# Loading w1 in two pieces, the small one first, and moving eight wo products to later gaps of TensorE

## Chip, cores, metric

The kernel runs on one core of one Trainium2 chip. The metric is the device time of one execution in microseconds (us), the median of several runs.

## The reference

One token goes through a gated mix of an attention block and a dense block. Only the last 4096 of 32768 cached keys and values are read.

```python
def reference(A_x, A_k_cache, A_v_cache, A_wq, A_wo, B_x, B_w1, B_b1, B_w2, B_b2, gate_w):
    x = A_x                                        # [1, 1, 576]
    g = sigmoid((x * gate_w).sum(-1, keepdims=True))
    # A: 32 query heads, 16 KV heads of 128, window W = 4096
    q = x @ wq;  p = softmax(q @ k[-W:].T * 128 ** -0.5);  a = (p @ v[-W:]) @ wo
    # B: 576 -> 4608 -> 576
    b = gelu(x @ w1 + b1) @ w2 + b2
    return g * a + (1 - g) * b
```

K and V of the window are 16.8 MB each, wq, wo, w1 and w2 5 MB each: 53.6 MB are read for a single token. (The code above is shortened; the kernel passes x for both blocks.)

## The kernel before

The parts that matter. All large loads go through one DMA queue, issued by SyncE (SP) in the order in which they are used; four small rows (x, the gate weights, b2, b1) go through a second queue, issued by ScalarE (ACT). The first SP load is moved ahead of everything else in the program.

```python
    nc.scalar.dma_start(out=x_row, ...)            # 1.1 KB each; b1_t two rows of 4.6 KB
    nc.scalar.dma_start(out=gw_row, ...)
    nc.scalar.dma_start(out=b2_row, ...)
    nc.scalar.dma_start(out=b1_t, ...)

    w1_t = big.tile([P, NI, FH], BF16, name="w1_t", tag="B")      # 128 x 9 x 2304
    w1_src = B_w1.rearrange("d (h n) -> (d h) n", h=2).rearrange("(p i) n -> p i n", i=NI)
    nc.sync.dma_start(out=w1_t[:], in_=w1_src)     # one row of 41,472 bytes per partition
    wq_t = ...                                     # one row of 36,864 bytes per partition
    # ... [cut: constants, x2 = x spread over the partitions, the gate g] ...
    for j in range(NJ): ...                        # h_ps  = b1 (18 matmuls)
    for i in range(NI):                            # h_ps += w1 (162 matmuls), i outermost
        for j in range(NJ):
            nc.tensor.matmul(h_ps[:, j:NF:NJ], lhsT=w1_t[:, i, j:FH:NJ], rhs=x2[:, i, :], ...)
    # ... [cut: gelu -> gt; q = wq x; K loads and transposes, scores; softmax; V loads, o] ...
    for r0, r1 in ((0, 16), (16, RO)):             # RO = 32
        nc.sync.dma_start(out=wo_t[:, r0:r1, :], in_=wo_src[:, r0:r1, :])
    for j0, j1 in ((0, 10), (10, 16), (16, 18)):   # second half of w2
        nc.sync.dma_start(out=w2_t[:, NJ + j0 : NJ + j1, :], in_=w2_src[:, 1, j0:j1, :])
    # ... [cut] ... y_add makes two matmuls, one for each half of the 576 outputs
    with tc.issue_after(ov_mm.ins):
        for f in range(6, NJ):
            y_add(gt[:, f : f + 1], w2_t[:, f, :])
    for r in range(RO):
        y_add(ov[:, r : r + 1], wo_t[:, r, :])
    for f in range(NJ, NF):
        y_add(gt[:, f : f + 1], w2_t[:, f, :], stop=(f == NF - 1))
    # out_row <- y (ScalarE and VectorE, one half each), then the store
```

## Time and profile before

| | before |
|---|---|
| time, median of 4 runs | 133.07 us (132.94 to 133.3) |
| span of the profiled run | 131.0 us |
| main DMA queue | 53.61 MB, packets 96.4% of 16 engines' span |
| x row lands / b1 rows are used | 7.4 / 15.5 us |
| h_ps done, q_ps done | 28.0, 31.85 us |
| last K, last V, last waited-for w2 landing | 66.4, 111.5, 128.2 us |

The first lines to read are those of the page: the 40 equal slices of the span (3.3 us each; a digit is tenths of the busy share or of the granted clock) and the line of the main DMA queue.

```profile
PEclk9999999999999999999999965555555555556999
DMA  7999899899999999999999999999999989999980
GB/s 215 481 470 456 362 439 450 356 435 425 420 430 425 425 425 430 430 425 425 440 424 492 400 420 470 410 410 460 425 400 455 460 375 400 433 427 419 407 329 26
...
q1 hardware_dynamic: 2882, 53.61, 96.4%
```

The DMA row is full, or nearly so (8 or 9), from the second slice to the last but one. The rate of 425 to 430 GB/s in the middle lies close to the fabric ceiling of 435 GB/s that the Trainium skill gives ("DMA: Bandwidth & Descriptors", Specifications); this trace agrees with that figure. TensorE, the busiest engine, is at 59%.

Next the chain of work that ended last, in order of time (start, duration, what; only some of its 67 pieces):

```profile
1.91 13.59 DMA rows<-in_B_b_dram
...
15.54 1.27 PE h_ps L304 x18
16.82 1.05 PE y_ps L290 x4
17.86 10.14 PE h_ps L316 x162
28.00 3.85 PE q_ps L354 x144
...
32.45 33.94 DMA k_t<-in_A_k_cache_dram
...
101.27 26.86 DMA w_t<-in_B_w_dram
...
128.17 1.20 PE y_ps L290 x16
```

A chain names one releaser for each wait. It names TensorE work (h_ps, q_ps) between two long DMA stretches, which looks as though a faster h_ps would help. It would not: behind q_ps the chain waits for K until 66.4 us. That K load is issued at 32.4 us, when a buffer comes free, and then stands 34 us in the DMA queue behind the loads issued before it.

The end of the timeline (start, duration, engine, line, what, count, and in brackets the idle time before it with its releaser):

```profile
116.70 3.04 PE L290 MATMUL y_ps<-w_t,gt 128*1 128x288 bf16 x24
...
119.53 2.63 PE L290 MATMUL y_ps<-wo_t,ov 128*1 128x288 bf16 x32
122.61 2.12 PE L290 MATMUL y_ps<-wo_t,ov 128*1 128x288 bf16 x32 [0.45 <-DMA wo_t<-in_A_wo_dram]
...
126.07 1.39 PE L290 MATMUL y_ps<-w_t,gt 128*1 128x288 bf16 x20 [1.34 <-DMA w_t<-in_B_w_dram]
...
128.17 1.15 PE L290 MATMUL y_ps<-w_t,gt 128*1 128x288 bf16 x16 [0.70 <-DMA w_t<-in_B_w_dram]
...
129.35 0.45 DVE L534 CAST out_row<-y_ps 1x288 bf16<-1x288 f32 x1 [12.36 <-PE y_ps L290]
```

TensorE waits three times for data at the end: 0.45, 1.34 and 0.70 us. After the last wait 16 matmuls remain (1.15 us), then the copies and the store.

### The profile page before, as it was taken

Reading aid. Unit: us, or ns where it says so; the run is one execution under the profiler, and the core shown is the slowest. Engines: PE = TensorE matmul, PEld = TensorE weight load, DVE = VectorE, ACT = ScalarE, POOL = GpSimd, SP = SyncE. Lnnn points to the kernel's source line nnn. Section 1 sums busy time; section 2 is a strip of 40 time slices with the busy share of each in tenths; the row PEclk is TensorE's granted clock in tenths of the full one; section 3 lists DMA queues with packets and bytes.
Section 4 is the critical chain, followed back from the end, with each engine's and each line's share of the span. In section 5 each row is a group of like instructions: output and inputs, shape, how many; then the busy total and the mean of one; then the engine's idle time right before and its main releaser. Section 6 shows DMA issues by size and latency. Waiting matters only on the chain.

```text
span 131.0 us, 2371 instructions
## 1 busy us (share of the span) xinstructions
PE 77.3 (59%) x1126; PEld 44.7 (34%) x1062; DVE 51.8 (40%) x48; ACT 13.0 (10%) x25; POOL 5.6 (4%) x25
## 2 busy tenths in 40 slices
PE   0021299998599778768768220004934730999853
PEld 0011279997112111111111010004934730955521
DVE  0025600034988988988986620736000000010001
ACT  2100000001200000000000029960000000000001
POOL 5004600000000000000000000000000000000000
PEclk9999999999999999999999965555555555556999
DMA  7999899899999999999999999999999989999980
GB/s 215 481 470 456 362 439 450 356 435 425 420 430 425 425 425 430 430 425 425 440 424 492 400 420 470 410 410 460 425 400 455 460 375 400 433 427 419 407 329 26
DMA packets 2900, 53.75 MB, mean 410 GB/s; under 512 B 326, under 2 KB 330, under 8 KB 588
## 3 DMA queue, kind: packets, MB, share of 16 engines
q1 hardware_dynamic: 2882, 53.61, 96.4%
q8 instruction: 8, 0.13, 0.4%
q10 hardware_dynamic: 10, 0.01, 0.0%
HBM read 53.62 MB, written 0.00 MB: 409 GB/s over the span
## 4 chain that ended last, share of the span: by engine, by line
DMA 57%; PE 22%; DVE 8%; ACT 8%; issue 3%; SPq 1%; ACTq 1%; DVEq 0%
DMA k_t<-in_A_k_cache_dram 26%; DMA w_t<-in_B_w_dram 20%; DMA rows<-in_B_b_dram 10%; PE h_ps L316 8%; ACT p_t L449 7%; PE o_ps L493 5%; DVE kt L397 3%; PE q_ps L354 3%; DVE pt L457 2%; DVE m L419 2%; PE y_ps L290 2%; PE s_ps L407 1%; PE h_ps L304 1%; SPq L506 1%; PE t_ps L473 0%
## 5 line engine op out<-in xcount | busy, mean ns | idle before, releaser
L397 DVE STREAM_TRANSPOSE kt<-k_t 128x2048 f32<-128x2048 f32 x16 | 36.0, 2290 | 4.9 <-DMA k_t<-in_A_k_cache_dram 4.9
L407 PE MATMUL s_ps<-kt,qz_flat 128*128 128x512 bf16 x128 | 32.0, 397 | 8.6 <-DVE kt L397 8.6
L493 PE MATMUL o_ps<-pt,v_t 128*128 128x8 bf16 x512 | 14.5, 168 | 10.0 <-DMA v_t<-in_A_v_cache_dram 7.3
L407 PEld LDWEIGHTS <-qz_flat 128*128 128x128 bf16 x64 | 6.4, 99 | 33.6 <-issue 33.6
L493 PEld LDWEIGHTS <-v_t 128*128 128x128 bf16 x512 | 14.3, 105 | 10.3 <-DMA v_t<-in_A_v_cache_dram 7.5
L449 ACT ACTIVATE p_t<-s_ps,negm 128x512 bf16<-128x512 f32 x8 | 9.7, 1410 | 44.2 <-DVE negm L440 44.2
L316 PEld LDWEIGHTS <-w_t 128*128 128x128 bf16 x162 | 10.1, 160 | 1.0 <-issue 1.0
L316 PE MATMUL h_ps<-x,w_t 128*128 128x2 bf16 x162 | 10.2, 202 | 0.0
L511 DVE TENSOR_TENSOR om<-o_ps,rgh 128x128 bf16<-128x128 f32 x1 | 0.3, 291 | 23.6 <-PE o_ps L493 23.6
L290 PE MATMUL y_ps<-w_t,gt 128*1 128x288 bf16 x72 | 7.2, 362 | 2.0 <-DMA w_t<-in_B_w_dram 2.0
L473 PE MATMUL t_ps<-ls,ones 128*128 128x32 f32 x2 | 0.6, 396 | 12.7 <-DVE ls L471 12.7
L457 DVE STREAM_TRANSPOSE pt<-p_t 128x2048 bf16<-128x2048 bf16 x2 | 4.6, 2312 | 7.4 <-ACT p_t L449 7.4
L239 PE MATMUL xs_ps<-one_b,rows 1*128 1x1 bf16 x9 | 0.7, 196 | 8.2 <-DVE rows L233 8.2
L534 DVE CAST out_row<-y_ps 1x288 bf16<-1x288 f32 x1 | 0.4, 446 | 12.4 <-PE y_ps L290 12.4
L290 PEld LDWEIGHTS <-gt 128*1 128x1 bf16 x72 | 3.6, 99 | 4.6 <-issue 2.5
L325 DVE COPY hacc<-h_ps 128x36 f32<-128x36 f32 x1 | 0.2, 196 | 12.3 <-PE h_ps L316 12.3
L290 PE MATMUL y_ps<-wo_t,ov 128*1 128x288 bf16 x64 | 4.8, 306 | 0.4 <-DMA wo_t<-in_A_wo_dram 0.4
L473 PEld LDWEIGHTS t_ps<-ls,ones 128*128 128x128 f32 x2 | 0.5, 309 | 12.8 <-issue 12.8
L533 ACT CAST out_row<-y_ps 1x288 bf16<-1x288 f32 x1 | 0.4, 390 | 42.0 <-PE y_ps L290 42.0
L354 PE MATMUL q_ps<-x,wq_t 128*128 128x2 bf16 x144 | 4.0, 166 | 0.0
L354 PEld LDWEIGHTS <-wq_t 128*128 128x128 bf16 x144 | 3.9, 104 | 0.0
L290 PEld LDWEIGHTS <-ov 128*1 128x1 bf16 x64 | 3.1, 91 | 2.2 <-issue 0.7
(65 smaller groups left out, 30.2 us busy)
## 6 DMA issues: line engine op xcount, KB each, us to landing
k_t<-in_A_k_cache_dram SPq DMA_DIRECT2D x8, 2048.0 KB, 32.7
v_t<-in_A_v_cache_dram SPq DMA_DIRECT2D x4, 4096.0 KB, 25.7
w_t<-in_B_w_dram SPq DMA_DIRECT2D x1, 5184.0 KB, 15.3
wq_t<-in_A_wq_dram SPq DMA_DIRECT2D x1, 4608.0 KB, 26.2
wo_t<-in_A_wo_dram SPq DMA_DIRECT2D x2, 2304.0 KB
w_t<-in_B_w_dram SPq DMA_DIRECT2D x1, 2592.0 KB, 11.3
w_t<-in_B_w_dram SPq DMA_DIRECT2D x1, 1440.0 KB, 25.2
w_t<-in_B_w_dram SPq DMA_DIRECT2D x1, 864.0 KB, 26.9
```

What stands on the lines that cost most here:

```text
L290: nc.tensor.matmul(y_out[s], lhsT=vec, rhs=row[:, s * DH : (s + 1) * DH], start=start, stop=stop, skip_group_check=True,)
L304: nc.tensor.matmul(h_ps[:, j:NF:NJ], lhsT=b1_t[:, j:FH:NJ], rhs=ident[0:2, 0:2], start=(j == 0), stop=False, skip_group_check=True,)
L316: nc.tensor.matmul(h_ps[:, j:NF:NJ], lhsT=w1_t[:, i, j:FH:NJ], rhs=x2[:, i, :], start=False, stop=(i == NI - 1 and j == NJ - 1), skip_grou ...
L354: nc.tensor.matmul(q_ps[:, j : Hq : Hq // 2], lhsT=wq_t[:, i, j * Dh : (j + 1) * Dh], rhs=x2[:, i, :], start=(i == 0 and j == 0), stop=(i ...
L397: nc.vector.transpose(out=kt[:, u * half : (u + 1) * half].bitcast(FP32), in_=k_t[:, f, u * SL // 2 : (u + 1) * SL // 2, :] .rearrange("p ...
L407: nc.tensor.matmul(s_ps[:, u * 512 : (u + 1) * 512].rearrange("p (c k) -> p c k", k=32), lhsT=qz[:, h0 // 2, j, :], rhs=kv[:, u * SL // 4 ...
L419: nc.vector.reduce_max(out=m2[:], in_=s_ps[:].rearrange("p (n b) -> p b n", b=2), axis=AX.X)
L449: nc.scalar.activation(out=p_t[:, cs, :, b], in_=s_ps[:].rearrange("p (c k u b) -> p u b c k", k=8, u=2, b=2)[:, f, b % 2], func=ACT.Exp, ...
L457: nc.vector.transpose(out=pt[:, cs, :].rearrange("p c h -> p (c h)"), in_=p_t[:, cs, :, :].rearrange("p c k b -> p (c k b)"),)
L473: nc.tensor.matmul(t_ps[:], lhsT=ones[:], rhs=ls[:], start=True, stop=True)
L493: v_last = nc.tensor.matmul(o_ps[:, 8 * g : 8 * g + 8, 0], lhsT=v_t[:, c, :], rhs=pt[:, c, 8 * g : 8 * g + 8], start=(c == 0), stop=(c == ...
L506: nc.sync.dma_start(out=wo_t[:, r0:r1, :], in_=wo_src[:, r0:r1, :])
```

## The change

The intent: let TensorE begin with w1 while most of w1 is still on its way, let the small rows in early, and fill the idle stretches at the end with wo products.

```diff
-    nc.sync.dma_start(out=w1_t[:], in_=w1_src)
+    for i0, i1 in ((0, 1), (1, NI)):
+        nc.sync.dma_start(out=w1_t[:, i0:i1, :], in_=w1_src[:, i0:i1, :])
...
-            nc.tensor.matmul(
+            last = nc.tensor.matmul(
...
+        return last
...
-    with tc.issue_after(ov_mm.ins):
-        for f in range(6, NJ):
-            y_add(gt[:, f : f + 1], w2_t[:, f, :])
-    for r in range(RO):
-        y_add(ov[:, r : r + 1], wo_t[:, r, :])
-    for f in range(NJ, NF):
-        y_add(gt[:, f : f + 1], w2_t[:, f, :], stop=(f == NF - 1))
+    late = [(gt, f, w2_t[:, f, :]) for f in range(6, NJ)]
+    wo_at = [(ov, r, wo_t[:, r, :]) for r in range(RO)]
+    w2_at = [(gt, f, w2_t[:, f, :]) for f in range(NJ, NF)]
+    late += wo_at[0:8] + wo_at[16:RO] + wo_at[8:13] + w2_at[0:10] + wo_at[13:16] + w2_at[10:]
+    before = ov_mm
+    for n, (vec, at, row) in enumerate(late):
+        with tc.issue_after(before.ins):
+            before = y_add(vec[:, at : at + 1], row, stop=(n == len(late) - 1))
```

## The prediction

> **What bounds the kernel now.** The DMA engines, nearly from end to end. The page: packets of the main queue took 96.4% of 16 engines' span (126.3 of 131.0 us). In the packet records w1's first packet starts 1.0 us in and the last w2 packet ends at 128.4 us; between, the engines are 99% occupied. The view by stretches: 412, 430 and 427 GB/s up to 38.6, 76.2 and 120.5 us, just under the 435 GB/s fabric ceiling of the Trainium skill ("DMA: Bandwidth & Descriptors", Specifications). After the last landing come 16 matmuls (1.15 us), two copies (0.45) and the store. The chain of waits names PE, ACT and DVE lines too, but the stream covers them: K lands last at 66.4, V at 111.5, w2 at 128.17, each when the queue gets there.
>
> **What the change does.**
> 1. w1 in two loads. The small ACT loads are taken one packet at a time between an engine's 41 KB packets (1.53 us each): x lands at 7.4, b1 at 15.5 us. Behind 4.6 KB packets (0.178 us, from b1's of that size) they should land 3 to 9 us earlier. TensorE then does b1 and the first 18 of 162 w1 products while it sat idle, the rest from w1's landing (about 15.4 instead of 17.8). h_ps (10.1 us) should end near 24.5 instead of 28.0; q_ps, held by wq (27.0), near 31 instead of 31.85. Off the critical path: DVE waits for K all through its stage.
>  Cost: 8 more packets per engine; 178 + 1364 ns (4608 and 36864 bytes) against 1533: 9 ns each, under 0.1 us in all, plus a covered issue (0.4 us). The first packets take about 0.8 us longer than later ones; I take that for filling the pipe whatever the size, so not recovered.
> 2. Order of the last products. TensorE idles 0.45 us for wo's second piece (122.6), 1.34 for ten w2 products (126.07), 0.70 for the last (128.17). Eight wo products (16 matmuls, 1.1 us) move into the last two gaps. The eight w2 products after the last landing stay, so the end stays landing plus 1.15 us plus copies and store; idle moves to before 122.6 us.
>
> **On the critical path:** almost nothing, -0.3 to +0.2 us.
>
> **Predicted time:** 132.9 us, 8 in 10 between 132.2 and 133.8. Chances: faster by over 2% 0.02, within 2% 0.93, slower 0.05.
>
> **What would show it.** x and b1 land early; h_ps done near 24.5; q_ps near 31; last K landing at 66 to 67, last V near 111; TensorE at its last wait with some 0.2 us left; last landing within 0.4 us of 128.2; total packet time within 0.2 us.
>
> **What would make it wrong.** (a) The granted clock: 0.5 from 76.2 to 120.5, full after. The skill ("TensorE: Matmul & The Clock Gate", Part 1) says some 3.4 us of sustained activity lifts the throttle; in the trace it lifts about 5 us after the y products start. If the new idle near 121 to 122.6 delays that, about 84 matmuls at 0.11 to 0.13 us instead of 0.07 end 2 to 3 us later. (b) Short first packets start the stream sooner: up to 0.8 us gained. (c) An uneven spread over the engines, whose last packets end over about 1.5 us. (d) One more completion semaphore in use delays a later issue until the queue empties; depth looks ample (10 to 20 us queued).

## The result and the profile after

| | before | after |
|---|---|---|
| time, median of 4 runs | 133.07 us | 132.74 us (132.5 to 132.85) |
| ratio, 95% interval | | 0.9971 (0.9948 to 0.9993) |
| span of the profiled run | 131.0 us | 131.1 us |
| x lands / b1 is used | 7.4 / 15.5 us | 3.7 / 13.6 us |
| h_ps done, q_ps done | 28.0, 31.85 us | 26.2, 31.2 us |
| last K, last V, last waited-for w2 landing | 66.4, 111.5, 128.2 us | 66.4, 111.7, 128.3 us |

By the 2% criterion the two kernels are the same; the difference, if it is one, is 0.3%.

The page of the kernel after, the lines that answer to those above:

```profile
PEclk9999999999999999999999985555555555558999
DMA  8999899899999999999999999999989999999980
GB/s 290 421 394 496 382 461 421 367 440 420 425 415 440 420 425 435 425 430 425 436 430 489 420 410 450 420 410 450 465 380 435 460 405 392 416 444 415 397 326 20
...
q1 hardware_dynamic: 3026, 53.61, 96.3%
```

Nothing has moved: the same bytes, the same full row. Its chain of work that ended last:

```profile
1.18 25.96 DMA wq_t<-in_A_wq_dram
...
27.19 4.01 PE q_ps L356 x144
...
31.80 34.56 DMA k_t<-in_A_k_cache_dram
...
101.44 26.80 DMA w_t<-in_B_w_dram
...
128.28 1.19 PE y_ps L291 x16
```

h_ps has left the chain; q_ps now waits for wq to land, and K still lands at 66.4 us. The head of the timeline shows what the two pieces did:

```profile
3.70 0.75 DVE L234 COPY rows<-rows 1x1152 bf16<-1x1152 bf16 x1 [3.70 <-DMA rows<-in_A_x_dram]
...
13.59 1.27 PE L306 MATMUL h_ps<-ident,rows 2*128 2x2 bf16 x18 [4.25 <-DMA rows<-in_B_b_dram]
...
14.80 1.28 PE L318 MATMUL h_ps<-x,w_t 128*128 128x2 bf16 x18
...
17.06 9.10 PE L318 MATMUL h_ps<-x,w_t 128*128 128x2 bf16 x144
26.19 0.20 DVE L327 COPY hacc<-h_ps 128x36 f32<-128x36 f32 x1 [14.94 <-PE h_ps L318]
...
27.19 4.00 PE L356 MATMUL q_ps<-x,wq_t 128*128 128x2 bf16 x144 [1.03 <-DMA wq_t<-in_A_wq_dram]
```

x is there 3.7 us earlier. b1 gains only 1.9 us. The first 18 w1 products (14.80) stand behind b1 in TensorE's order and so start only just before the rest of w1 lands (15.3 us). They save nothing: from b1's first product to the end of h_ps TensorE takes 12.5 us before (15.54 to 28.00) and 12.6 us after (13.59 to 26.19). The 1.8 us by which h_ps ends earlier come from b1's earlier landing. Then TensorE waits 1.03 us for wq.

The end of the timeline, after:

```profile
116.87 2.56 PE L291 MATMUL y_ps<-w_t,gt 128*1 128x288 bf16 x24
...
119.26 1.15 PE L291 MATMUL y_ps<-wo_t,ov 128*1 128x288 bf16 x16
122.69 2.74 PE L291 MATMUL y_ps<-wo_t,ov 128*1 128x288 bf16 x42 [2.28 <-DMA wo_t<-in_A_wo_dram]
...
126.16 1.39 PE L291 MATMUL y_ps<-w_t,gt 128*1 128x288 bf16 x20 [0.73 <-DMA w_t<-in_B_w_dram]
...
127.38 0.54 PE L291 MATMUL y_ps<-wo_t,ov 128*1 128x288 bf16 x6
...
128.28 1.14 PE L291 MATMUL y_ps<-w_t,gt 128*1 128x288 bf16 x16 [0.36 <-DMA w_t<-in_B_w_dram]
```

The wait near 122 grew from 0.45 to 2.28 us, those at 126 and 128 shrank to 0.73 and 0.36 us. The same 16 matmuls stand behind the last landing. So the moved products turned idle time near the end into idle time a little earlier, and nothing else.

### The profile page after: what moved, and what is told of

Read it like the earlier page. It is cut to its first block, busy times and chain, and to the rows that moved or that the text cites. A ratio compares the mean times of both kernels' runs of the same rounds, so it can differ in the third digit from the quotient of the medians.

```text
span 131.1 us, 2372 instructions
## 1 busy us (share of the span) xinstructions
PE 77.1 (59%) x1126; PEld 44.5 (34%) x1062; DVE 50.3 (38%) x48; ACT 12.9 (10%) x25; POOL 5.9 (4%) x25
## 4 chain that ended last, share of the span: by engine, by line
DMA 67%; PE 12%; DVE 8%; ACT 8%; issue 3%; SPq 1%; DVEq 0%
DMA k_t<-in_A_k_cache_dram 26%; DMA w_t<-in_B_w_dram 20%; DMA wq_t<-in_A_wq_dram 20%; ACT p_t L451 7%; PE o_ps L495 5%; DVE kt L399 3%; PE q_ps L356 3%; DVE pt L459 2%; DVE m L421 2%; PE s_ps L409 1%; PE y_ps L291 1%; SPq L508 1%; PE t_ps L475 0%; DVE out_row L537 0%; SPq L510 0%
## 5 line engine op out<-in xcount | busy, mean ns | idle before, releaser
L409 PE MATMUL s_ps<-kt,qz_flat 128*128 128x512 bf16 x128 | 32.7, 404 | 8.5 <-DVE kt L399 8.5
L291 PE MATMUL y_ps<-w_t,gt 128*1 128x288 bf16 x72 | 6.7, 345 | 1.1 <-DMA w_t<-in_B_w_dram 1.1
L306 PE MATMUL h_ps<-ident,rows 2*128 2x2 bf16 x18 | 1.3, 198 | 4.2 <-DMA rows<-in_B_b_dram 4.2
```

Source lines behind the costliest of these rows:

```text
L291: last = nc.tensor.matmul(y_out[s], lhsT=vec, rhs=row[:, s * DH : (s + 1) * DH], start=start, stop=stop, skip_group_check=True,)
L306: nc.tensor.matmul(h_ps[:, j:NF:NJ], lhsT=b1_t[:, j:FH:NJ], rhs=ident[0:2, 0:2], start=(j == 0), stop=False, skip_group_check=True,)
L409: nc.tensor.matmul(s_ps[:, u * 512 : (u + 1) * 512].rearrange("p (c k) -> p c k", k=32), lhsT=qz[:, h0 // 2, j, :], rhs=kv[:, u * SL // 4 ...
```

## The experiments

A difference of 0.3% needs experiments with many runs. Each kernel below was run six times beside eleven runs of the kernel before on the same chip. The theories at the start were:

- A: the gain is real and comes from the head of the DMA stream, because of w1's split. A1, its narrower form: shorter first rows fill the DMA pipe sooner.
- B: it comes from the new order of the last products.
- C: it is chance.
- D: any split of w1 does it. E and F: the early small rows, or TensorE's earlier start, do it.

One number of the trace is used throughout, the *lag*: at 20 us after the start, the time minus the bytes moved so far (from the packet records) divided by the rate of 16 engines at 41,472 bytes per 1533 ns, the duration of a w1 row in the kernel before in steady flow. It says by how many us the stream is behind an ideal one that started at zero.

### Which part, if any: four kernels on one chip

The control is the kernel before itself.

> The kernel before against itself, to see how large a ratio chance alone gives. Every theory expects 1.000 within its interval; if it is 0.997 or 1.003 with an interval that leaves out 1, then the 0.3% of the change is not to be explained at all.

Measured: 133.01 us, ratio 1.0007 (0.9994 to 1.0021). The control differs by 0.07%, and its interval reaches 0.2%.

Only the split of w1:

```diff
-    nc.sync.dma_start(out=w1_t[:], in_=w1_src)
+    for i0, i1 in ((0, 1), (1, NI)):
+        nc.sync.dma_start(out=w1_t[:, i0:i1, :], in_=w1_src[:, i0:i1, :])
```

> Only the split of w1, the order of the last products as before. Theory A (the 0.3% comes from the head of the DMA stream: shorter first packets, 0.60 us of extra packet time in the first 5 us instead of 0.77[...]): ratio 0.997 to 0.998. Theory B (it comes from the order of the last products): 1.000 or 1.001, for 128 more packets at 9 ns. Theory C (no effect, drift of the runs): 1.000.

Measured: 132.66 us, ratio 0.9983 (0.9971 to 0.9996).

Only the new order of the last products, w1 in one load:

```diff
-    for r in range(RO):
-        y_add(ov[:, r : r + 1], wo_t[:, r, :])
-    for f in range(NJ, NF): ...
+    late += wo_at[0:8] + wo_at[16:RO] + wo_at[8:13] + w2_at[0:10] + wo_at[13:16] + w2_at[10:]
+    ... (as in the change)
```

> Only the order of the last products, w1 in one load. Theory A: 1.000, TensorE idles before 122.6 us instead of before 126 and 128 us, and the 16 products behind the last landing still take 1.15 us. Theory B: 0.997. Theory C: 1.000.

Measured: 133.0 us, ratio 1.0003 (0.9989 to 1.0017). Its profile shows the idle time before 122.43 us (1.60 us) and the 16 matmuls after the last wait, 1.15 us, as before.

The whole change again:

> The whole change again on this chip. Theories A and B: 0.997 as on record, its interval leaving out 1. Theory C: 1.000 within 0.2%, like the control.

Measured: 132.71 us, ratio 0.9982 (0.9971 to 0.9994).

Theory B falls. The split alone gives what the change gives, 0.2%, and both intervals leave out 1, so C is unlikely (the two share the same eleven runs of the kernel before, so they are not two independent proofs). These are 0.2 to 0.25 us of 133.

### Is the DMA stream the bound from start to end?

A wrong result: one ninth of w1 is not loaded, TensorE's work stays.

```diff
-    for i0, i1 in ((0, 1), (1, NI)):
+    for i0, i1 in ((0, 1), (1, NI - 1)):
...
-                lhsT=w1_t[:, i, j:FH:NJ],
+                lhsT=w1_t[:, min(i, NI - 2), j:FH:NJ],
```

> A wrong result on purpose: one row of nine of w1 (0.59 MB) is not loaded, the products of that row read the row before, so TensorE's work is the same. If the DMA stream bounds the kernel from start to end, the time falls by 8 packets of 4.6 KB per engine, 8 x 171 ns = 1.37 us against the change: ratio to the kernel before 0.988. If TensorE, DVE or the softmax chain bound some stage, it falls by less, down to 0.998.

Measured: 131.18 us, ratio 0.9864 (0.984 to 0.9888). The end of its timeline:

```profile
126.62 1.15 PE L291 MATMUL y_ps<-w_t,gt 128*1 128x288 bf16 x16 [0.36 <-DMA w_t<-in_B_w_dram]
...
127.80 0.45 DVE L537 CAST out_row<-y_ps 1x288 bf16<-1x288 f32 x1 [12.40 <-PE y_ps L291]
```

Bytes left out in the first 15 us arrive in full at the end: the last wait ends at 126.62 instead of 128.28 us. That is 1.66 us, somewhat more than the 1.37 us of the missing bytes; in this profile the packets of the first 5 us also took 0.41 us longer than their steady time, against 0.60 us in the profile of the change. Against the second profile of the change (128.19 us) the saving is 1.57 us. No later stage takes the gain back, so none of them bounds the kernel, at least not within these 1.7 us.

### Big piece first, and other first pieces

The 37 KB rows first:

```diff
-    for i0, i1 in ((0, 1), (1, NI)):
+    for i0, i1 in ((0, NI - 1), (NI - 1, NI)):
```

> The change with the two pieces of w1 the other way round: the 37 KB rows first, then the 4.6 KB rows. As many packets as the change. Theory A1 (the 0.2% is the shorter first packet: the extra time of the packets of the first 5 us, 0.76 us in the three profiles with one load, 0.57 in those with the small piece first): ratio 1.000 to 1.001, the extra time back near 0.75 us. Theory D (any split of w1 does it, by the added packets, the shifted issues or the earlier h_ps): ratio 0.998.

Measured: 132.82 us, ratio 0.9988 (0.9963 to 1.0012). Inconclusive: the interval holds both expectations. The lag was 1.98 us. Two of the eleven runs of the kernel before took 133.46 and 133.78 us beside it, which lowers the ratio; the medians, 132.82 and 132.88 us, are all but equal. This kernel also bears on theory F: b1 is used at 13.74 us and h_ps ends at 26.2 us, as with the change, though x lands only at 7.8 us.

A tiny first piece, 1.15 KB of each partition's w1:

```diff
-    for i0, i1 in ((0, 1), (1, NI)):
-        nc.sync.dma_start(out=w1_t[:, i0:i1, :], in_=w1_src[:, i0:i1, :])
+    w1_f, w1_s = (a.rearrange("p i n -> p (i n)") for a in (w1_t[:], w1_src))
+    for n0, n1 in ((0, 576), (576, NI * FH)):
+        nc.sync.dma_start(out=w1_f[:, n0:n1], in_=w1_s[:, n0:n1])
```

> The change with a first piece of 1.15 KB rows (8 packets of about 51 ns per engine) and a second of 40 KB rows. Theory A1: extra time of the first packets at most that of the change, about 0.5 us, ratio 0.997 to 0.999, unless the engines run dry before the second load, issued 0.8 us in, reaches them. Theory E (the gain comes with the small ACT loads, which need the 1.4 us of small packets to get in between): x lands after a 40 KB packet, near 5 us or later, and the ratio is 1.000.

Measured: 133.9 us, ratio 1.0072 (1.0037 to 1.0108). Slower. The reservation in the expectation came true: by the packet records the engines were occupied for 0.57 of the second microsecond and 0.84 of the third, then 1.0; the change has 0.71 and 1.0. The second load was issued at about 0.8 us and was not yet flowing when eight packets of some 51 ns were through. The lag was 2.54 us, 0.6 to 0.7 us more than with the whole change, but the time is 1.2 us longer. In the profile wo's second piece is waited for until 0.56 us later than with the change (123.25 against 122.69 us), the last w2 piece until 1.06 us later (129.34 against 128.28): half of the loss arose in the last 6 us of the stream, and no run here shows why. One expectation was plainly wrong: x landed at 2.2 us, earlier than in any other kernel. That did not help, which speaks against E, but weakly, as the loss could hide a gain of 0.2 us.

The next four ran together on one chip. Three of the eleven runs of the kernel before took 133.8 us there, at the same granted clocks as the others; I have no cause for them, and they widen the intervals and lower the ratios. So neighbours are compared with each other too. By the medians, which such runs move less, the ratios of the first three below are 0.998, 1.001 and 0.998. The whole change:

> The whole change a third time, as the neighbour of the next three on one chip. Theory A1 (the gain is a shorter fill of the DMA stream): ratio 0.998; the stream some 1.87 us behind an ideal one after 20 us, against 1.97 with one load of w1. Theory C (chance): 1.000.

Measured: 132.78 us, ratio 0.9971 (0.9939 to 1.0003), lag 1.87 us.

Big piece first again:

> The 37 KB rows first again, since the first try (0.9988, 0.9963 to 1.0012) told nothing apart. Theory A1: ratio 0.9995 to 1.001, above the run beside it, lag 1.97 us. Theory D (any split does it): like the run beside it, 0.998, lag 1.87.

Measured: 133.11 us, ratio 0.9989 (0.9957 to 1.0021), lag 2.01 us. The interval again holds 1 and 0.998. Beside its neighbour the six runs are slower: 132.87 to 133.25 us against 132.64 to 133.08.

Two rows of w1 first (9.2 KB), then 32 KB:

```diff
-    for i0, i1 in ((0, 1), (1, NI)):
+    for i0, i1 in ((0, 2), (2, NI)):
```

> A first piece of 9.2 KB rows, a second of 32 KB. Theory A1, if the fill grows with the first row's size: between the change and big-first, 0.9985, lag 1.9 us. If only running dry and rows over 30 KB matter: as good as the change or better, 0.998.

Measured: 132.75 us, ratio 0.9964 (0.9933 to 0.9996), lag 1.93 us. Its six runs (132.55 to 132.84) lie below all six of big-first. It cannot be told from the change, so it is no better version. Its lag lies with the kernels that load w1 in one piece (1.93 to 2.00), while its time is that of the change: here lag and time disagree, which does not support A1.

### Everything early, but more packets

All of w1 in one load of 4.6 KB rows; the tile is padded so that the nine rows of a partition are not joined into one:

```diff
-    w1_t = big.tile([P, NI, FH], BF16, name="w1_t", tag="B")
+    w1_t = big.tile([P, NI, FH + 16], BF16, name="w1_t", tag="B")
...
-    for i0, i1 in ((0, 1), (1, NI)):
-        nc.sync.dma_start(out=w1_t[:, i0:i1, :], in_=w1_src[:, i0:i1, :])
+    nc.sync.dma_start(out=w1_t[:, :, 0:FH], in_=w1_src)
```

> All of w1 in one load of 4.6 KB rows (the tile padded, so that rows are not joined): 72 packets per engine where the change has 16. The b1 row should land before 8 us instead of 13.6, h_ps should end near 26 or earlier, and all this is off the critical path. Theory A1 with the cost of 9 ns per packet predicted for the change: 56 more packets per engine cost 0.5 us against the change, ratio to the kernel before 1.001 to 1.003. Theory F (the early small loads and the earlier TensorE are what gains): 0.996 or less.

Measured: 133.86 us, ratio 1.0051 (1.0016 to 1.0086). Slower than expected. The head of its timeline:

```profile
8.27 1.24 PE L305 MATMUL h_ps<-ident,rows 2*128 2x2 bf16 x18 [0.26 <-POOL ident masks.py:199]
...
15.91 10.21 PE L317 MATMUL h_ps<-x,w_t 128*128 128x2 bf16 x162 [5.32 <-DMA w_t<-in_B_w_dram]
26.16 0.20 DVE L326 COPY hacc<-h_ps 128x36 f32<-128x36 f32 x1 [16.74 <-PE h_ps L317]
```

TensorE works on b1 at 8.27 us, 5.3 us earlier than with the change (what it waited for last was a constant of GpSimd, no longer b1), then waits 5.32 us for w1 as a whole, and h_ps ends at the same 26.2 us. Not everything is early: x lands at 5.9 us, later than with the change (3.7). Theory F gets no support: the earliest b1 of all goes with one of the slowest kernels, and big-first, with the change's b1 and h_ps, shows no gain clear of noise. A gain hidden by this kernel's longer lag is not excluded. The lag is 2.74 us, 0.87 more than the change's 1.87, and the trace divides it: the first packet starts at 1.44 instead of 1.02 us (the issue itself took 0.67 us instead of 0.40), and between 4 and 20 us the lag grows from 2.38 to 2.74, that is 0.36 us for 56 more packets per engine, 6.4 ns each (in the neighbouring profile of the change the lag does not grow there). The remaining 0.09 us arises before 4 us.

This profile also shows the risk that the prediction named under (a). The end of its timeline, and stretches of it (us, then busy time of PE, PEld, DVE, ACT and POOL with counts, the granted clock, DMA share and GB/s):

```profile
120.36 1.15 PE L290 MATMUL y_ps<-wo_t,ov 128*1 128x288 bf16 x16
123.49 4.41 PE L290 MATMUL y_ps<-wo_t,ov 128*1 128x288 bf16 x42 [1.98 <-DMA wo_t<-in_A_wo_dram]
...
127.73 1.39 PE L290 MATMUL y_ps<-w_t,gt 128*1 128x288 bf16 x20
```

```profile
120.20:123.60 3.40, 1.42 (x24) 0.86 (x20) 0.00 (x0) 0.00 (x0) 0.00 (x0) 1.00 0.96 405
123.60:127.00 3.40, 3.40 (x32) 1.94 (x30) 0.00 (x0) 0.00 (x0) 0.00 (x0) 0.50 0.98 405
127.00:130.50 3.50, 3.47 (x56) 2.29 (x52) 0.00 (x0) 0.00 (x0) 0.00 (x0) 0.99 0.36 145
```

During the idle stretch that the new order makes larger, the granted clock fell back to a half for 3.4 us, and the 42 matmuls after it took 4.41 us instead of 2.74. TensorE then worked without a wait to the end: its last 16 matmuls start 1.04 us later than with the change (129.32 against 128.28 us), where V and wo are waited for until 0.8 us later, so some 0.2 us of this profile's end may come from the clock. It is hardly what makes the kernel slower: the two of its six runs with the highest mean clock (0.845) took 133.84 and 133.89 us. The fall happened in one of the eleven profiles with the new order. That the idle time caused it was not tested; gaps of up to 2.73 us (big-first and the next kernel) did not bring it.

### Fewer products behind the last landing

```diff
-    for j0, j1 in ((0, 10), (10, 16), (16, 18)):
+    for j0, j1 in ((0, 13), (13, 17), (17, 18)):
...
-    late += ... + wo_at[8:13] + w2_at[0:10] + wo_at[13:16] + w2_at[10:]
+    late += ... + wo_at[8:13] + w2_at[0:13] + wo_at[13:16] + w2_at[13:]
```

> The change with the second half of w2 in pieces of 13, 4 and 1 products instead of 10, 6 and 2, so that 5 products (10 matmuls) and not 8 (16) stand behind the last waits. If the end is the landing plus the products behind it: 6 matmuls at 0.07 us less, up to 0.4 us, ratio 0.995 to 0.997. If the last piece of all lands later than the wait shown, less: 0.997 to 0.998.

Measured: 133.09 us, ratio 1.0005 (0.9979 to 1.0032). A miss: the change alone had 0.997 to 0.998 in its three measurements. The end of its timeline:

```profile
126.95 1.76 PE L291 MATMUL y_ps<-w_t,gt 128*1 128x288 bf16 x26 [1.80 <-DMA w_t<-in_B_w_dram]
...
128.54 0.54 PE L291 MATMUL y_ps<-wo_t,ov 128*1 128x288 bf16 x6
...
128.91 0.78 PE L291 MATMUL y_ps<-w_t,gt 128*1 128x288 bf16 x10
```

A piece of 13 lands 0.8 us later than one of 10. From 126.95 us TensorE has 42 matmuls without a pause, to 129.7 us, so the last pieces find it busy and no wait shows. The end is the later of two things, the landing plus what stands behind it, and the last long wait plus all of the products after it. My expectation had only the first.

## Why the prediction was right

The predicted 132.9 us and "within 2%" held; 132.74 was measured. Point by point:

- *DMA bounds the kernel from end to end.* Right, and shown: leaving out 0.59 MB at the head (1.4 us of packets) saved 1.7 us against the kernel before. x 5 us earlier (tiny first) and b1 7 us earlier (all small rows) went with slower kernels, and h_ps 2 us earlier (big-first) with no gain clear of noise.
- *The order of the last products is worth nothing.* Right: 1.0003 alone. Idle moved to before 122.7 us, TensorE reached its last wait 0.36 us ahead of the data (0.2 predicted).
- *x, gate, b1 land 3 to 9 us earlier.* Half right. x gained 3.7 us, b1 only 1.9. The step assumed that all four rows would go in between the 4.6 KB packets. Those are over about 3 us after the start, and the later rows arrived behind 37 KB packets. On the ACT queue's records one engine shows x at 3.1, then data and completions at about 5.9, 7.4, 8.7, 10.1, 11.5 and 13.0 us: each takes a turn after one 37 KB packet of 1.36 us, where before it was one of 1.53 us. In the big-first kernel, without small packets at the head, b1 is used at 13.74 us: this points to the 37 KB rows, not the small piece, as the source of its gain.
- *h_ps ends near 24.5.* Wrong by 1.7 us, from the same step: the 18 early products stand behind b1, at 13.6 us, and the rest of w1, there at 15.3 us (15.4 predicted), waits behind them and the b2 products until 17.06 us. It cost nothing, as h_ps is off the critical path; q_ps, held by wq until 27.2 us, ended at 31.2 (31 predicted).
- *The first packets' extra 0.8 us is a fill whatever the row's size, so not recovered.* Mis-sized, it seems; the prediction had the other case as its risk (b), and its -0.3 to +0.2 us on the critical path holds the 0.2 to 0.25 us found in the experiments (0.33 in the first measurement). By the packets of the first 5 us, the extra time over their steady durations was 0.69 to 0.81 us in three profiles with one load, 0.55 to 0.60 in four with the small piece first (0.49 and 0.41 in the two others, with the w2 pieces changed and with less of w1) and 0.71 and 0.79 in two with the big piece first. The lag says the same in other terms: 1.93 to 2.00 us with one load, 1.96, 1.87, 1.87 and 1.87 with the small piece first (1.85 and 1.78 in the two others), 1.98 and 2.01 with the big one first. So about 0.1 us of lag is recovered, net of the additional packets.
- *Cost of the additional packets, 9 ns each.* About right: 6.4 ns in the kernel with 56 more.

What stays open: the split's gain in time is 0.2 to 0.25 us by the means of six runs, with intervals from 0.05 to 0.4; the lag could account for 0.1 of it. For the shorter fill as the cause speaks that big-first loses it in the trace and, beside its neighbour, in time (133.11 against 132.78 us). Against it speak the two-rows kernel, fast with a lag of 1.93, and the profiled runs themselves, whose lag does not order their spans: the kernel before 131.0 us with a lag of 2.00, the control 131.4 with 1.93, the change 131.1 with 1.96. So the cause of the 0.2% is not shown, and whether all of it is real these runs can't say.

## What to carry to other kernels

In this kernel, whose one DMA queue is full from the second microsecond to nearly the last, the time moved with three things: the bytes and (a little) the packets, when the stream starts and fills, and what stands behind the last long waits. Work that started earlier elsewhere, and products moved between gaps, only moved idle time about. A small first piece must still be large enough to keep the engines fed until the second load flows: 4.6 KB and 9.2 KB rows were; the kernel with 1.15 KB rows lost 1.0 us against the kernel before, 0.6 of it at the head of the stream. Judge a tail by two sums, landing plus the rest behind it and the last long wait plus all the work after it.

## What the Trainium skill lacked or had wrong

- "DMA: Bandwidth & Descriptors", Queues, rings and completion order: it says that an engine drains a packet of typically 9 to 17 descriptors of one queue before it switches. Here the switch came after every single 41 KB or 37 KB row: the ACT queue's records on one engine are 1.5 us apart before (5.29, 6.87, 8.40, 9.98 us) and 1.3 to 1.5 us after, and data and completion each took a turn. That a small row beside large ones waits for two such turns is not said.
- The same page, Bandwidth: it says that for HBM to SBUF the limit of about 358 GB/s per core binds. This one core moved 427 to 430 GB/s for most of its span. The sentence lacks the condition that the same section states elsewhere, both cores of a pair streaming; its single-core figure of 425 GB/s fits.
- The same page, Latency and other measured facts: it gives a first byte after about 0.6 us on this path, but not from where that is counted. Here the first packet started 1.02 us after the issue began, which is 0.62 us after the issue ended, and with 72 rows per engine instead of 8 it started after 1.44 and 0.77 us. That the issue grows with the number of rows (0.40 to 0.67 us) has no line for this path.
- No page says how the first packets' fill depends on the row size: 0.69 to 0.81 us of extra packet time with 41 KB rows first, 0.41 to 0.60 with 4.6 KB rows first.
- "TensorE: Matmul & The Clock Gate", HAM oscillation: it states the rule of no idle gaps over about 3.4 us. In one profile the granted clock fell to a half for 3.4 us after a gap of 1.98 us, in a stretch of 3.4 us with 1.42 us of matmul time; gaps of 2.28 and 2.39 us in the profiles of the change, and of 2.73 us in two others, did not bring that.
